# A fused attention and MLP kernel: the last 64 tokens of the first batch moved from the start into stage 2 of tile 0, and the first w_in transfer cut in halves

## The chip, the cores and the metric

The kernel runs on one core of one Trainium2 chip. The metric is the device time of one execution in microseconds (us). A ratio of a kernel is the mean time of its fast runs over the mean time of the fast runs of the kernel before in the same rounds on the same chip, so it is not quite the ratio of the medians that stand beside it; the brackets hold its 95% interval. The experiments ran on several chips, so I compare their ratios.

Engines: PE multiplies matrices (PEld is its weight load), DVE is VectorE, ACT is ScalarE, POOL is GpSimd, SP issues transfers. A transfer has *landed* when the last of its sixteen completions is recorded in the trace.

## The reference

```python
# q, k, v: (8 batches, 8 heads, 576 tokens, 64) f32; w_in: (512, 2048); w_out: (2048, 512)
scores = scale * np.matmul(q, k.transpose(0, 1, 3, 2))
mask = (rel >= 0) & (rel < 64)              # each token sees itself and the 63 before
...                                          # softmax
x = np.matmul(attn, v).transpose(0, 2, 1, 3).reshape(4608, 512)
h = x @ w_in
g = h * np.clip(h + 3.0, 0.0, 6.0) / 6.0
out = g @ w_out
```

The 4608 tokens are worked on in nine tiles of 512. Stage 1 of a tile is `x @ w_in` with the gate, stage 2 is the product with `w_out`. A batch has 576 tokens, 64 more than a tile: the last 64 tokens of batch 0 ("the rest") belong to tile 1.

## The kernel before

PE is given one fixed list of work, in which the attention of the next batch is laid between pieces of the two stages. Only the start and tiles 0 and 1 matter here.

```python
# loads of batch 0 by SP: q and k by pairs of heads, then the rest of q and k, then V
for h0 in range(0, H, 2):
    ...                                   # q, k of heads h0, h0 + 1, tokens 0:512
    if h0 == 2:                           # the rest: tokens 512:576 of all heads
        for i, src in enumerate((q, k)):
            nc.sync.dma_start(out=rst[i*SR:(i+1)*SR], in_=src[0, :, SM:S, :]...)
# POOL: casts to bf16, and w_in in four parts of 512 columns, which cast while they move
bt.cast_v_end(vst0, pcopy)
bt.cast_v(vst0, 0, 2, pcopy)
w_in = []
for i in range(4):
    w_in.append(load_w_in(512 * i, 512 * (i + 1), 0, NG))
    if i < 3:
        bt.cast_v(vst0, 2 * i + 2, 2 * i + 4, pcopy)
...
# w_out in four parts behind w_in; batch 1's V behind the third of them
for x in insv:
    after(x, w_out[2], "the weights go first")
...
# stage 2 of tile 0: m yields one piece (four matmuls 128x512) at a time
run(m, 2)
masked(bt, 3)
run(m, 2)
for g in range(NG):        # four pairs of heads of batch 1
    run(m, 1)
    N_(bt, g)              # value matmuls (PE), normalisation (DVE)
    run(m, 1)
    if g:
        X_(bt, g - 1)      # transposes (PE), copy into x (ACT)
run(m)
```

`SS(b, g)` in the list of pieces below stands for the scores of a pair of heads, with exponentials on ACT and the mask on DVE; the number in front is the piece of stage 2 after which it comes.

The softmax here doesn't subtract the row's maximum and nothing guards it: scores larger than these inputs give would overflow.

## Time and profile before

| | |
|---|---|
| time, median of 3 | 316.76 us (315.65 to 317.39) |
| span of the profiled execution | 312.9 us (its run took 314.71) |
| PE busy | 298.8 us, 96% |
| stage 1 of tile 0 starts, last w_out part landed | about 20.6 us, 46.68 us |
| stage 1 of tile 1 starts, stage 2 of tile 1 starts, stage 1 of tile 2 starts | 59.7, 74.3, 93.8 us |

The profile is read from the start: PE is full from 39 us on, so what counts is when its list of work gets to a place, and which transfer or copy it waits for there. The prediction shows the lines. The profiled execution was a quick one (314.71 us against a median of 316.76), so differences between traces come out about 1 us larger than those between medians.

### The profile page before, as it was taken

To read this page: it belongs to the slowest core of one execution; us is meant where nothing else is said; L and a number is where in the kernel's file an instruction comes from. 1 tells how busy PE (TensorE), PEld (TensorE's weight loads), DVE (VectorE), ACT (ScalarE), POOL (GpSimd) and SP (SyncE) were. 2 spreads that over 40 slices of the span, in tenths; PEclk is the share of its full clock that TensorE was granted. 3 is DMA by queue.
4 is the path that set the end of the run, shared out by engine and by line. 5 is a ranking of instruction groups with operands and counts; after the bars stand their busy time and mean duration, and the time that the engine had idled before them with its cause. 6 is when DMAs were issued, how large, how long until landed. Compare 5 with 4: busy or idle time off the path is not lost.

```text
span 312.9 us, 5589 instructions
## 1 busy us (share of the span) xinstructions
PE 298.8 (96%) x2126; PEld 149.0 (48%) x2162; DVE 174.5 (56%) x331; ACT 177.2 (57%) x264; POOL 86.1 (28%) x131
## 2 busy tenths in 40 slices
PE   7879799999999999999999999999999999999995
PEld 3444444544554455445544554455445544444442
DVE  4557753476646765477447853785377627306700
ACT  3648753378637854696158715881588157317611
POOL 5840805363036143306500750165000000000000
PEclk9999999999999999999999999999999999999998
DMA  8999999998899999999999999999900630010011
GB/s 212 241 180 250 250 203 196 205 185 245 187 195 212 272 214 205 229 228 216 195 248 202 207 199 239 212 198 186 242 4 2 128 93 0 34 69 34 0 69 67
DMA packets 151516, 52.80 MB, mean 169 GB/s; under 512 B 138945, under 2 KB 147137, under 8 KB 151489
## 3 DMA queue, kind: packets, MB, share of 16 engines
q1 hardware_dynamic: 146672, 46.94, 73.5%
q0 software_dynamic: 4544, 5.24, 9.2%
q8 instruction: 17, 0.28, 0.4%
q10 hardware_dynamic: 272, 0.26, 0.2%
q14 instruction: 11, 0.08, 0.1%
HBM read 36.70 MB, written 9.44 MB: 147 GB/s over the span
## 4 chain that ended last, share of the span: by engine, by line
PE 88%; ACT 3%; DMA 3%; SPq 2%; DVE 1%; issue 1%; POOL 1%
PE o L503 20%; PE acc L503 19%; PE hT L466 18%; PE st L466 8%; PE acc L466 6%; PE o L466 6%; PE st L347 4%; PE hT L377 2%; PE hT L382 2%; DMA qst<-in_q_dram 1%; PE hT L407 1%; DMA vst<-in_v_dram 1%; ACT pT L355 1%; DVE gT L474 1%; SPq L82 1%
## 5 line engine op out<-in xcount | busy, mean ns | idle before, releaser
L466 PEld LDWEIGHTS <-win 128*128 128x128 bf16 x576 | 55.4, 98 | 66.9 <-issue 1.0
L503 PEld LDWEIGHTS <-gT 128*128 128x128 bf16 x576 | 52.8, 98 | 57.6 <-issue 0.4
L503 PE MATMUL o<-wout,gT 128*128 128x512 bf16 x277 | 68.1, 379 | 0.8 <-issue 0.2
L503 PE MATMUL acc<-wout,gT 128*128 128x512 bf16 x275 | 66.1, 379 | 0.8 <-issue 0.2
L466 PE MATMUL hT<-xT,win 128*128 128x512 bf16 x267 | 64.9, 379 | 0.3
L355 ACT ACTIVATE pT<-st 128x768 bf16<-128x768 f32 x64 | 48.8, 810 | 15.1 <-PE st L347 15.0
L474 DVE SCALAR_TENSOR_TENSOR gT<-t,st 128x512 bf16<-128x512 bf16 (+1 forms) x26 | 19.7, 768 | 56.6 <-ACT t L473 56.5
L473 ACT ACTIVATE t<-hT,half 128x512 bf16<-128x512 f32 x68 | 46.1, 691 | 8.8 <-PE hT L466 8.6
L474 DVE SCALAR_TENSOR_TENSOR gT<-t,hT 128x512 bf16<-128x512 bf16 x68 | 46.0, 685 | 8.6 <-ACT t L473 8.4
L365 DVE TENSOR_TENSOR pT<-pT,mask 128x1536 bf16<-128x1536 bf16 x28 | 28.2, 1006 | 16.3 <-ACT pT L355 16.3
L252 POOL CAST qn<-qst 128x512 bf16<-128x512 f32 x24 | 15.7, 695 | 71.4 <-DMA qst<-in_q_dram 71.4
L509 ACT COPY osb<-acc 128x512 f32<-128x512 f32 x18 | 10.6, 587 | 39.2 <-PE acc L503 39.2
L509 ACT COPY osb<-o 128x512 f32<-128x512 f32 x18 | 10.6, 588 | 35.4 <-PE o L503 35.4
L466 PE MATMUL st<-xT,win 128*128 128x512 bf16 x116 | 27.9, 379 | 1.4 <-ACT xT L412 0.8
L397 DVE TENSOR_TENSOR opg<-hT,rec 128x320 bf16<-128x320 f32 x56 | 27.5, 492 | 1.9
L466 PE MATMUL acc<-xT,win 128*128 128x512 bf16 x91 | 23.6, 379 | 0.1
L466 PE MATMUL o<-xT,win 128*128 128x512 bf16 x90 | 23.5, 379 | 0.1
L473 ACT ACTIVATE t<-st,half 128x512 bf16<-128x512 f32 (+1 forms) x26 | 19.4, 752 | 6.0 <-PE st L466 5.9
L377 PEld LDWEIGHTS <-pT 128*128 128x128 bf16 x256 | 17.9, 97 | 9.6 <-issue 2.0
L394 DVE RECIPROCAL rec<-hT 128x5 f32<-128x5 f32 x56 | 10.6, 189 | 19.0 <-PE hT L386 18.8
L243 POOL CAST V<-vst 128x512 bf16<-128x512 f32 (+1 forms) x14 | 16.3, 1167 | 16.2 <-DMA vst<-in_v_dram 9.8
L347 PE MATMUL st<-QT,KT 64*128 64x192 bf16 (+2 forms) x320 | 17.9, 229 | 2.7 <-ACT KT L316 1.5
(76 smaller groups left out, 267.1 us busy)
## 6 DMA issues: line engine op xcount, KB each, us to landing
out_dram<-osb SPq DMA_DIRECT2D x32, 256.0 KB, 2.4
qst<-in_q_dram SPq DMA_DIRECT2D x28, 256.0 KB, 4.9
kst<-in_k_dram SPq DMA_DIRECT2D x27, 256.0 KB, 5.7
vst<-in_v_dram SPq DMA_DIRECT2D x24, 256.0 KB, 5.3
vst<-in_v_dram SPq DMA_DIRECT2D x24, 128.0 KB, 4.4
win<-in_moe_w_in_dram POOLq DMA_DIRECT2D x4, 512.0 KB, 7.8
wout<-in_moe_w_out_dram POOLq DMA_DIRECT2D x4, 512.0 KB, 8.5
qst<-in_q_dram SPq DMA_DIRECT2D x2, 512.0 KB, 5.3
```

What stands on the lines that cost most here:

```text
L243: copy(out=self.V[:, 0 : KB - 1, h0:h1, 0:D], in_=vst[:, 0 : KB - 1, h0:h1, :])
L252: pcopy(out=n[:, g, 0 : KB - 1, :, :].rearrange("p k h d -> p k (h d)"), in_=s[:, 0 : KB - 1, 2 * g : 2 * g + 2, :].rearrange("p k h d -> ...
L347: nc.tensor.matmul(st[:, h, o0 : o0 + n], lhsT=bt.KT[h * D : (h + 1) * D, g, k0 : k0 + P], rhs=bt.QT[h * D : (h + 1) * D, g, q0 : q0 + n], ...
L355: nc.scalar.activation(out=pT[:, :, 2 * u : 2 * u + 2, 0:QW], in_=st[:, :, 0:w].rearrange("p h (k w) -> p h k w", k=2), func=EXP, scale=scale,
L365: nc.vector.tensor_tensor(out=pT[:, :, :, 0:QW], in0=pT[:, :, :, 0:QW], in1=mask[:].rearrange("p (h k) w -> p h k w", h=2), op=MULT,)
L377: nc.tensor.matmul(ob, lhsT=pT[:, h, qb, 0:P], rhs=V[:, qb, 2 * g + h, :], start=True, stop=(qb == 0),)
L397: nc.vector.tensor_tensor(out=opgs[bt.b, g][:, :, h, :], in0=ov[:, :, 0:D], in1=rec[:].unsqueeze(2).to_broadcast([P, KB, D]), op=MULT,)
L466: nc.tensor.matmul(hT, lhsT=win16[:, g, fc * P : (fc + 1) * P], rhs=xT[:, g, t0 : t0 + TB], start=(g == 0), stop=(g == NG - 1),)
L473: nc.scalar.activation(out=t1[:], in_=hT, func=RELU, bias=half[:], scale=1.0 / 6.0)
L474: nc.vector.scalar_tensor_tensor(out=out, in0=t1[:], scalar=1.0, in1=hT, op0=MIN, op1=MULT,)
L503: nc.tensor.matmul(accs[ts], lhsT=gT[:, fc, ts * P : (ts + 1) * P], rhs=wout16[:, fc, :], start=(fc == 0), stop=(fc == NFC - 1),)
L509: nc.scalar.copy(out=osb[:], in_=accs[ts])
```

## The change

Its intent: stage 1 can start when the attention of batch 0 is done; without the last 64 tokens there are three loads, six casts and some matmuls fewer in front of it. The rest's attention is done later, in a place where PE works on stage 2 of tile 0. The first w_in part comes in two halves so that stage 1 can start with the first. The loads of batch 2 come later, so its scores do, too.

```diff
@@ loads of batch 0: the rest and the V tail leave the start @@
-            if h0 == 2:
-                for i, src in enumerate((q, k)):
-                    nc.sync.dma_start(out=rst[...], in_=src[0, :, SM:S, :]...)
+    def load_rest_of_first():        # issued in front of batch 1's V
+        for dst, p0, src in ((rst, 0, q), (rst, SR, k), (rvst, SR, v)): ...
@@ POOL at the start @@
-        if g == 1:
-            bt.cast_rest(st, pcopy)
-    bt.cast_v_end(vst0, pcopy)
     bt.cast_v(vst0, 0, 2, pcopy)
-    w_in = []
-    for i in range(4):
-        w_in.append(load_w_in(512 * i, 512 * (i + 1), 0, NG))
-        if i < 3:
-            bt.cast_v(vst0, 2 * i + 2, 2 * i + 4, pcopy)
+    bt.cast_v(vst0, 2, 4, pcopy)
+    w_in = [load_w_in(0, 512, 0, 2)]
+    bt.cast_v(vst0, 4, 6, pcopy)
+    w_in.append(load_w_in(0, 512, 2, NG))
+    bt.cast_v(vst0, 6, 8, pcopy)
+    w_in += [load_w_in(512 * i, 512 * (i + 1), 0, NG) for i in (1, 2, 3)]
@@ POOL in stage 2 of tile 0, in front of batch 1's V @@
+    bt0.cast_rest((None, None, rst0), pcopy)
+    pcopy(out=bt0.V[SR:P, KB - 1, :, 0:D], in_=rvst0[SR:P, :, :])
+    pcopy(out=bt0.V[0:SR, KB - 1, :, 0:D], in_=bt0.V[SR:P, KB - 2, :, 0:D])
     bt.cast_v_end(vst1, pcopy)
@@ PE in stage 2 of tile 0 @@
     masked(bt, 3)
-    run(m, 2)
+    later[0, "r"] = bt0.rest_t(...)      # 4 transposes
+    do(bt0, "r")
+    run(m, 1)
+    rest_s(bt0)                          # 8 score matmuls
     for g in range(NG): ...
+        if g == 0:
+            rest_n(bt0)                  # 8 value matmuls
+        if g == 1:
+            rest_x(bt0)                  # 4 transposes
@@ batch 2 in stage 2 of tile 1 @@
-                0: [f(SS, 0)], 1: [f(SS, 1)], 3: [f(N_, 0), f(SS, 2)], 5: [f(X_, 0)],
-                6: [f(N_, 1), f(SS, 3)], 8: [f(X_, 1)], 9: [f(N_, 2)], 11: [f(X_, 2)],
-                12: [f(N_, 3)], 14: [f(X_, 3)],
+                1: [f(SS, 0)], 2: [f(SS, 1)], 4: [f(N_, 0), f(SS, 2)], 6: [f(X_, 0), f(SS, 3)],
+                7: [f(N_, 1)], 9: [f(X_, 1)], 10: [f(N_, 2)], 12: [f(N_, 3), f(X_, 2, 0)], 14: [f(X_, 3, 1)],
... (removal of the rest from the matmuls of batch 0, other cuts)
```

## The prediction

> **What bounds the kernel now.** I read the page first, to see which engine fills the span.
>
> ```profile
> PE 298.8 (96%) x2126; PEld 149.0 (48%) x2162; DVE 174.5 (56%) x331; ACT 177.2 (57%) x264; POOL 86.1 (28%) x131
> PE   7879799999999999999999999999999999999995
> ```
>
> TensorE (PE) is busy 96% of the span. Its only slices (7.8 us each) under 9 tenths are four of the first five and the last. So from about 39 us on the end can move only if PE's whole stream starts earlier or loses gaps; time is to be had at the start. There I read the chain of waits in order of time.
>
> ```profile
> 3.72 0.04 issue
> 3.76 4.53 DMA qst<-in_q_dram
> ...
> 11.88 3.75 DMA vst<-in_v_dram
> 15.63 0.70 POOL win L222
> ...
> 18.19 0.63 POOL V L243
> ...
> 18.86 0.22 PE o L377 x2
> ...
> 19.97 0.65 ACT xT L412
> 20.62 0.16 issue
> 20.78 1.67 PE st L466 x7
> ```
>
> Up to 20.8 us the end is set by loads of q, then of v, then by GpSimd (POOL), which casts V and issues the w_in loads in turn. L466 is the first matmul of stage 1 of tile 0; from there the chain is PE. The list of waits adds what the chain hides: the weight load of that matmul waited for w_in itself. The chain shows seven matmuls there where the program has eight, so one record is missing, and I take 20.55, where the timeline has the weight load, as the start.
>
> ```profile
> PEld L466 <- DMA win<-in_moe_w_in_dram: 0.8, 1, 0.8
> ```
>
> Then I asked whether the DMA engines have room, by stretches of the start.
>
> ```profile
> 2.00:45.00 43.00, 37.08 (x331) 19.52 (x333) 26.58 (x64) 26.53 (x40) 20.43 (x32) 1.00 1.15 234
> ```
>
> The last two numbers are the DMA share and GB/s. A share of 1.15 over 43 us means that they never rest before 45 us. So everything up to the last w_out load is one queue of bytes, and I checked how closely PE follows it. The last w_out is issued at 37.88, and the view of that tile gives:
>
> ```profile
> DMA to landing us min/median/max: 7.0/8.5/8.8
> ```
>
> With the largest it lands at 46.7. PE begins the part that reads it (u=3 of the first block) at 46.76 in the timeline. The third part has landed by 44.02, when SP issues batch 1's V, which waits for it; PE uses it at 44.48. PE is at the heels of the weights.
>
> **What the Trainium skill says.** "DMA: Bandwidth & Descriptors", Specifications: transfers under 512 B fall short of line rate. The trace agrees: between 8 and 9 us, with 1 KB runs of q and k, 351 GB/s; between 12 and 13 us, with 256 B runs of v, 219. The last 64 tokens are loaded in 256 B runs, so each of their three loads (131 KB) costs about 0.6 us of the DMA engines. Same page, "Issuing engines are not separate DMA queues": all queues run on the same 16 engines. So a load that moves is not saved; it delays what it is put in front of. "Runtime: NRT & Kernel Launch", Instruction fetch mechanics: instructions arrive in 16 KiB blocks of 256. The page agrees (instruction queue: 17 packets, 0.28 MB). PE's third fetch here is at 46.8 us, and SP's issue of a V load at 46.98 then took 1.74 us instead of 0.51; a fetch can hit the new loads. "TensorE: Matmul & The Clock Gate", part 2: only weight loads are pulled ahead, matmuls stay in order. The trace shows the same, so a rest matmul that waits holds everything behind it.
>
> **The change part by part.**
> (1) Loads. Out of the start go two rst loads and the V tail: 3 x 131 KB / 219 GB/s = 1.8 us of DMA time, and 0.73 + 0.62 + 0.61 us of SP's issue. The third q pair, issued at 3.76, goes out at 2.32; V follows it. V should land 1.8 us earlier.
> (2) POOL. The casts of rn (0.62) and V's end (0.61) and the four half-tile casts (0.29 each) leave: 2.4 us. The last V cast, 18.19 before, falls to about 15.5 (V data 1.8 earlier, one 0.3 tail less per round, and each w_in issue of 0.75 still between casts).
> (3) PE, VectorE and ScalarE of the start: per head pair one score pair, two of 16 value matmuls and one of 5 transposes fewer, and normalisation over 256 columns instead of 320 (0.49 to about 0.4). None was the last wait; four rounds of about 1.2 us from the first V cast put PE at the door of stage 1 at about 17.4.
> (4) w_in in halves. Before, the first part was issued at 13.72 and landed in 6.8 us. V's data end near 13.5-14 now; half a moves half the bytes, about 1.3 us less, so it lands near 17.5 and half b near 19.2, in time for the (2,) group. Stage 1 starts about 2.9 us earlier. But parts 1, 2, 3 are now all issued after the last V cast, and behind them the stream is earlier only by about 1.25 us: 1.8 us of bytes less what the later issues and the slow start of the software queue lose.
> (5) What becomes of the 2.9. Batch 1's first heads (cast waiting for w_in part 2, then k at 32.4), then w_out 0 to 3, all ride on the stream, so PE catches up with it: w_out 1 would be needed at 41.55 - 2.4 = 39.2 and lands near 40.2. By the last w_out, where there was no slack (46.7 against 46.76), PE's gain is the stream's: X = 1.25 us, between 0.8 and 1.8.
> (6) The rest in stage 2 of tile 0. PE work: 4 transposes 0.3, 8 scores 0.27, 8 value matmuls 0.27, 4 transposes 0.15, together 0.9 to 1.0 us, inserted where PE is the path (the same work removed at the start was not). Waits: the casts of rst0 end about 4.9 us after w_out 2 (two loads at 3.5 and 4.1 us, cast 0.62), PE wants them at 4.55: 0.35 lost, against 0.25 before at the same spot for the o bank. Batch 1's V comes three loads (1.8 us) later while PE reaches N(0) with two pieces done instead of three: 0.2 to 1.2 us lost. To the good: one piece of stage 2 is left for the last head pair, which closes the 0.39 us wait on the xT copy at 58.76 and some of the other 0.8 us of stalls there. Net: about +0.5 us (-0.1 to +1.3).
> (7) Batch 2's loads are behind the three new ones: 1.8 - 1.25 = about 0.6 us later than before. K's transpose of pair 0 landed at 74.8 and PE wanted it at 75.28. One piece (0.86 us) later it is wanted as late as it comes; no stall over 0.3. The last transposed outputs taking the score banks are neutral.
> After that PE's stream is the same.
> Sum: -1.25 + 0.5 = -0.75, so 316.76 - 0.75 = 316.0.
>
> **The rivals.**
> - *The whole start is kept* (2 to 3 us faster, near 314). For it: stage 1 does start that much earlier. Against: the DMA share of 1.15 to 45 us, and w_out landing 0.1 us before use.
> - *The rest's loads take the gain back or more* (317 to 318). For it: V of batch 1 was cast from 49.92 (waiting 1.72 us for its data) for a use at 51.33, so little slack absorbs 1.8 us of loads; a fetch may add 1.2 to 2 us to one load. Against: PE has its own work between, and N(1) to N(3) come later than their casts.
> - *POOL starves the DMA queues*: with V's last pair hit by a fetch, parts 1 to 3 of w_in are issued a microsecond later and a gap opens; X falls to 0.8 or less and PE waits in stage 1 at its fifth block. Time about 316.5.
>
> **Range and chances.** X's spread of 0.5 and the insertion's 0.6 make about 0.8; the three runs before spread 315.65 to 317.39, which adds 0.6 to a median. An 80% range of 1.3 to 1.4 either side: 314.6 to 317.3. Two per cent is 6.3 us, which nothing here reaches: faster 0.01, within 2% 0.98, slower 0.01.
>
> **What would show it.** Right: L466's first matmul at about 17.6 instead of 20.6; a new PE wait for w_in part 1 or w_out 0/1 in stage 1 or at the start of stage 2; the last w_out landing near 45.4 instead of 46.7; the rn0 cast within half a microsecond of PE's wish; stage 1 of tile 1 starting at about 59.0 instead of 59.7; from there the same stream. Wrong: w_out landing 2 us or more earlier (then the first rival), a PE wait over 1.5 us for V or rn0 in stage 2 (the second), a DMA share under 1 between 14 and 20 us (the third), or a stall at batch 2's scores over 0.5 us.

## The result and the profile after

The kernel after takes 319.99 us in the median (319.07 to 320.56, 4 runs) against 316.72 us (315.65 to 317.39, 4 runs): ratio 1.0104 [1.0063, 1.0144]. It is about 3.3 us slower, outside the predicted range of 314.6 to 317.3 us. Executions over 1.5% slower than the fastest of the same kernel are left out of the means. The profiled execution has a span of 317.2 us (run 319.07).

The top of the page hardly shows it:

```profile
PE 301.3 (95%) x2125; PEld 148.7 (47%) x2162; DVE 176.4 (56%) x336; ACT 178.2 (56%) x266; POOL 87.5 (28%) x129
PE   7879699999989999999999999999999999999995
PEclk9999989999999999999999999999999999999999
```

PE is busy 2.5 us longer, though it has no more work. The last row is its granted clock, and the 8 in the sixth slice means that the clock was reduced for a part of it; before, only the last slice had an 8. I come back to this.

The chain of waits up to the start of stage 1 of tile 1, in order of time (start, duration, what):

```profile
15.76 9.59 DMA win<-in_moe_w_in_dram
...
27.15 6.69 DMA rst<-in_k_dram
...
35.24 9.55 DMA wout<-in_moe_w_out_dram
...
46.14 3.45 DMA rvst<-in_v_dram
...
49.70 0.62 POOL V L727
50.37 1.12 POOL V L728
...
51.66 0.62 POOL V L252
52.34 0.62 POOL V L247
53.04 0.35 POOL V L249
53.44 0.19 PE hT L394
```

Before, no transfer and no POOL operation stood in this chain from 20.8 us on; it was PE with some steps of ACT and DVE, and came to the first value matmuls of batch 1 so:

```profile
48.74 2.75 PE o L503 x12
51.49 0.06 PE hT L377 x2
```

Now it runs through w_in, batch 1's own loads and w_out until 44.8 us, then through the load of the rest's V (rvst) and five operations of POOL, of which the first two (L727, L728) are the rest's, to a value matmul of batch 1 at 53.44. The last transfer named (rvst) and the first two casts are work that the change put there.

Next, where the stream of weights lost its time. Busy time by microsecond (the last three numbers of a line are granted clock, DMA share and GB/s), after and then before:

```profile
14.00:15.00 1.00, 0.98 (x22) 0.68 (x22) 0.43 (x3) 1.00 (x2) 1.00 (x2) 1.00 0.79 109
15.00:16.00 1.00, 0.54 (x13) 0.45 (x14) 0.93 (x5) 0.60 (x2) 1.00 (x3) 1.00 1.01 132
16.00:17.00 1.00, 0.81 (x18) 0.55 (x15) 0.96 (x4) 0.52 (x1) 1.00 (x2) 1.00 0.90 97
17.00:18.00 1.00, 0.87 (x13) 0.69 (x15) 0.93 (x4) 0.39 (x2) 0.26 (x1) 1.00 1.08 119
18.00:19.00 1.00, 1.00 (x6) 0.45 (x5) 0.96 (x5) 0.26 (x1) 0.00 (x0) 1.00 0.67 80
20.00:21.00 1.00, 0.75 (x4) 0.40 (x5) 0.00 (x0) 0.27 (x1) 0.00 (x0) 1.00 1.25 209
```

```profile
16.00:17.00 1.00, 0.44 (x11) 0.36 (x8) 0.93 (x4) 0.94 (x2) 0.84 (x2) 1.00 0.98 140
17.00:18.00 1.00, 0.84 (x20) 0.76 (x20) 0.53 (x3) 0.11 (x1) 0.94 (x3) 1.00 1.15 189
18.00:19.00 1.00, 0.36 (x10) 0.28 (x7) 0.96 (x3) 0.64 (x1) 0.89 (x3) 1.00 1.15 170
```

After the change, from 14 to 19 us, only w_in is moving, and it moves at 80 to 132 GB/s where the same queue does some 205 from 20 us on. (These are bytes as written, in bf16.) Before, where its first packets come at 15.3 us, the queue starts slowly too (140), but is at 170 to 189 two microseconds later; after, it takes five. PE then waits for w_in in stage 1, in the list of waits up to 40 us (total us, times, longest):

```profile
PEld L524 <- DMA win<-in_moe_w_in_dram: 2.0, 2, 1.2
...
PE hT L524 <- DMA win<-in_moe_w_in_dram: 0.7, 1, 0.7
```

These two rows overlap in part, since PE and its weight load wait together. The view of the w_out tile after ends with the line that answers to the one in the prediction:

```profile
DMA to landing us min/median/max: 7.7/8.8/9.8
```

The transfers' times in us:

| | before | after | after minus before |
|---|---|---|---|
| stage 1 of tile 0 starts | 20.6 | 17.75 | -2.8 |
| first w_in part landed | 20.50 | 17.47 and 20.20 (halves) | -0.3 |
| w_in parts 2, 3, 4 landed | 23.01, 25.61, 28.15 | 22.79, 25.35, 27.89 | -0.2, -0.3, -0.3 |
| last w_out part landed | 46.68 | 47.40 | +0.7 |
| stage 1 of tile 1 starts | 59.7 | 62.7 | +3.0 |
| stage 2 of tile 1 starts | 74.3 | 77.6 | +3.3 |
| stage 1 of tile 2 starts | 93.8 | 98.0 | +4.2 |
| end | 312.9 | 317.2 | +4.3 |

So stage 1 of tile 0 starts as early as predicted, and by the last w_out part all is lost. Another 2.3 us go between that and stage 1 of tile 1, and 1.0 in stage 2 of tile 1. (One matmul record of eight is missing at the start of stage 1 of tile 1 before, so it began some 0.2 us earlier than 59.7; what seems lost in the stage itself is that.) From 98 us on the two traces run side by side.

The POOL timeline of stage 2 of tile 0, before and after (start, duration, line, operation, out and in, what it waited for):

```profile
49.92 0.62 POOL L243 CAST V<-vst 128x512 bf16<-128x512 f32 x1 [1.72 <-DMA vst<-in_v_dram]
```

```profile
48.93 0.61 POOL L293 CAST rn<-rst 128x512 bf16<-128x512 f32 x1 [8.77 <-DMA rst<-in_k_dram]
49.70 0.62 POOL L727 CAST V<-rvst 64x512 bf16<-64x512 f32 x1 [0.16 <-DMA rvst<-in_v_dram]
50.37 1.24 POOL L728 COPY V<-V 64x512 bf16<-64x512 bf16 x1
51.66 0.61 POOL L252 CAST V<-vst 64x512 bf16<-64x512 f32 x1
52.34 0.62 POOL L247 CAST V<-vst 128x512 bf16<-128x512 f32 x1
```

Before, POOL waited for the data; batch 1's first V cast began at 49.92. After, the data of that pair has landed at 51.42, but POOL has not got through the rest's three operations and the end of V; the cast begins at 52.34.

Stage 2 of tile 1, after: the timelines of DVE and of PE.

```profile
88.69 0.96 DVE L371 TENSOR_TENSOR pT<-pT,mask 128x1536 bf16<-128x1536 bf16 x1 [1.86 <-ACT pT L361]
89.57 0.19 DVE L402 RECIPROCAL rec<-hT 128x5 f32<-128x5 f32 x1
...
90.42 0.49 DVE L405 TENSOR_TENSOR opg<-hT,rec 128x320 bf16<-128x320 f32 x1
```

```profile
90.97 0.45 PE L416 MATMUL hT<-ident,opg 128*128 128x128 bf16 x5 [1.00 <-DVE opg L405]
```

DVE masks the fourth pair's scores, for which it waited for ACT's exponentials until 88.69, and only then normalises the second pair, whose value matmuls PE had finished before. PE's transposes wait 1.00 us. In the order of before the fourth scores stood behind those value matmuls; there is no such wait in that trace.

From these views I had three theories: (A) the halves slow the queue; (B) the insertion costs 2 to 2.5 us, mostly through POOL and the loads in front of batch 1's V; (C) the place of the fourth scores costs 1 us. The rivals were that POOL's issues are late, that one copy of 1.24 us is the cost, and, from the clock row, that a slow PE clock is.

### The profile page after: what moved, and what is told of

It is laid out like the page before. It is cut to its first block, busy times and chain, and to the rows that moved or that the text cites.

```text
span 317.2 us, 5591 instructions
## 1 busy us (share of the span) xinstructions
PE 301.3 (95%) x2125; PEld 148.7 (47%) x2162; DVE 176.4 (56%) x336; ACT 178.2 (56%) x266; POOL 87.5 (28%) x129
## 4 chain that ended last, share of the span: by engine, by line
PE 78%; DMA 12%; POOL 2%; ACT 2%; SPq 2%; DVE 2%; issue 2%; POOLq 0%
PE acc L561 18%; PE o L561 17%; PE hT L524 17%; PE acc L524 6%; PE o L524 6%; PE st L524 5%; PE st L353 3%; DMA win<-in_moe_w_in_dram 3%; DMA wout<-in_moe_w_out_dram 3%; DMA rst<-in_k_dram 2%; PE hT L383 2%; PE hT L388 1%; DMA qst<-in_q_dram 1%; DMA rvst<-in_v_dram 1%; PE hT L416 1%
## 5 line engine op out<-in xcount | busy, mean ns | idle before, releaser
L561 PE MATMUL o<-wout,gT 128*128 128x512 bf16 x276 | 68.8, 382 | 1.0 <-issue 0.5
L371 DVE TENSOR_TENSOR pT<-pT,mask 128x1536 bf16<-128x1536 bf16 x28 | 29.1, 1040 | 17.9 <-ACT pT L361 17.8
L531 ACT ACTIVATE t<-st,half 128x512 bf16<-128x512 f32 (+1 forms) x26 | 19.4, 752 | 7.1 <-PE st L524 7.1
L383 PEld LDWEIGHTS <-pT 128*128 128x128 bf16 x256 | 17.6, 97 | 8.7 <-issue 0.9
L247 POOL CAST V<-vst 128x512 bf16<-128x512 f32 (+1 forms) x14 | 16.4, 1168 | 15.7 <-DMA vst<-in_v_dram 12.8
L257 POOL CAST kn<-kst 128x512 bf16<-128x512 f32 x24 | 14.9, 658 | 19.1 <-DMA kst<-in_k_dram 19.1
L353 PE MATMUL st<-QT,KT 64*128 64x192 bf16 (+2 forms) x312 | 17.6, 230 | 1.9 <-ACT KT L321 1.5
```

The costliest lines, as they stand in the source:

```text
L247: copy(out=self.V[:, 0 : KB - 1, h0:h1, 0:D], in_=vst[:, 0 : KB - 1, h0:h1, :])
L257: pcopy(out=n[:, g, 0 : KB - 1, :, :].rearrange("p k h d -> p k (h d)"), in_=s[:, 0 : KB - 1, 2 * g : 2 * g + 2, :].rearrange("p k h d -> ...
L353: nc.tensor.matmul(st[:, h, o0 : o0 + n], lhsT=bt.KT[h * D : (h + 1) * D, g, k0 : k0 + P], rhs=bt.QT[h * D : (h + 1) * D, g, q0 : q0 + n], ...
L371: nc.vector.tensor_tensor(out=pT[:, :, :, 0:QW], in0=pT[:, :, :, 0:QW], in1=mask[:].rearrange("p (h k) w -> p h k w", h=2), op=MULT,)
L383: nc.tensor.matmul(ob, lhsT=pT[:, h, qb, 0:P], rhs=V[:, qb, 2 * g + h, :], start=True, stop=(qb == 0),)
L531: nc.scalar.activation(out=t1[:], in_=hT, func=RELU, bias=half[:], scale=1.0 / 6.0)
```

## The experiments

All gave correct results. Each edit is shown against the kernel that is named. Several expectations missed the time: whole gained more and halves_only cost more than forecast, and no gain came that could be told from noise in after_warm, after_ss3, rest_v_late, rest_v_warm and rest_v_warm_ss3.

| kernel | median us (runs) | before | ratio |
|---|---|---|---|
| whole | 317.1 (6) | 316.43 | 1.0024 [1.0009, 1.0039] |
| old_scores | 318.24 (6) | 316.43 | 1.0071 [1.0052, 1.0091] |
| copy_early | 318.65 (6) | 316.43 | 1.0094 [1.0065, 1.0124] |
| halves_only | 319.51 (5) | 316.43 | 1.0113 [1.0094, 1.0132] |
| whole_old | 316.48 (6) | 316.61 | 0.9997 [0.9958, 1.0037] |
| after_warm | 320.05 (6) | 316.61 | 1.0113 [1.0067, 1.0158] |
| late_half | 318.94 (6) | 316.61 | 1.0065 [1.0023, 1.0107] |
| rest_v_late | 317.12 (6) | 316.61 | 1.0016 [0.9971, 1.0061] |
| rest_v_warm | 316.77 (6) | 316.33 | 1.0016 [0.9976, 1.0056] |
| before_warm | 316.47 (6) | 316.33 | 1.0002 [0.9961, 1.0042] |
| halves_in_a_row | 319.28 (6) | 316.33 | 1.0098 [1.0048, 1.0149] |
| halves_by_columns | 319.21 (6) | 316.33 | 1.0081 [1.0042, 1.0121] |
| first_in_quarters | 319.63 (4) | 316.44 | 1.0107 [1.0084, 1.0130] |
| second_in_halves | 318.97 (4) | 316.44 | 1.0093 [1.0061, 1.0125] |
| halves_then_two | 319.97 (4) | 316.44 | 1.0120 [1.0092, 1.0147] |
| rest_v_warm_ss3 | 316.52 (22) | 316.44 | 1.0010 [0.9990, 1.0030] |
| scores_only | 317.33 (22) | 316.41 | 1.0031 [1.0013, 1.0048] |
| after_ss3 | 319.26 (6) | 316.41 | 1.0095 [1.0066, 1.0124] |

### The halves of the first w_in part

**whole** (against after) and **halves_only** (against before):

```diff
# whole                                          # halves_only: the change's POOL order
-    w_in = [load_w_in(0, 512, 0, 2)]
+    w_in = [load_w_in(0, 512, 0, NG)]
     bt.cast_v(vst0, 4, 6, pcopy)
-    w_in.append(load_w_in(0, 512, 2, NG))
```

(halves_only is before with the seven lines of the change from `cast_v(vst0, 2, 4)` to `w_in +=`, and nothing else. These lines also move the issues behind the casts of V.)

> The changed kernel with the first w_in part whole again, issued where half a was (after the second V cast). Theory A (the two halves are what makes the software queue crawl between 14 and 19 us, at some 110 GB/s where it later moves 205): the DMA share from 14 to 19 us is above 1.1, w_in part 2 lands near 24 instead of 25.35 us, stage 1 has no wait for w_in over 0.3 us after its start, the start of stage 1 is at 18.5 to 19.5 instead of 17.7; the time falls by 0.5 to 1.3 us against the changed kernel, to about 319. Theory B (the crawl is from the three w_in issues in a row, or from the cold queue): the share stays under 1.1 for 4 us or more, part 2 lands at 25 or later, and the time is that of the changed kernel, 320, within 0.5.

> The kernel before with only the w_in part of the change: first part in two halves, issued after the second and third V cast, parts 1 to 3 after the fourth. Theory A (halves make the software queue crawl): DMA share under 1.1 for 4 us after the first w_in packets, w_in part 2 lands later than 25.6 us, by 0.5 to 1.5 us, PE waits for w_in in stage 1, time 317.0 to 318.2. Theory B (halves are harmless): part 2 lands at 25.6 within 0.4, time 316.3 to 317.0.

The windows of whole:

```profile
14.00:15.00 1.00, 1.00 (x23) 0.75 (x22) 0.43 (x3) 1.00 (x2) 0.95 (x2) 1.00 0.62 71
15.00:16.00 1.00, 0.53 (x11) 0.38 (x11) 0.96 (x4) 0.68 (x2) 1.00 (x2) 1.00 1.24 208
18.00:19.00 1.00, 1.00 (x6) 0.49 (x5) 0.96 (x5) 0.33 (x1) 0.00 (x0) 1.00 1.24 207
```

The queue is at full rate from 15 us on, with the same casts on POOL around the issues. The whole first part landed at 17.73, hardly later than the first half in after; stage 1 started at 17.77, PE's weight load waited 0.2 us for w_in in all, and the last w_out landed at 45.10, 1.6 us earlier than before. This is the best of the traces with a whole first part: in five others of the kernels below the part landed at 18.1 to 19.1 us and PE's weight load waited up to 1.3 us for w_in, so a little was there for the halves to win. Theory A is shown, and larger than I had put down. Between whole and after lie 0.8 of a per cent, 2.5 us, with intervals that do not meet; old_scores and whole_old below, which also differ in nothing but the halves, lie 0.74 of a per cent apart, 2.3 us. The traces agree: the last w_out landed at 47.1 to 48.6 us in all nine kernels with the change's start and a split first part, and at 45.1 to 46.3 in whole, whole_old, rest_v_late and rest_v_warm (47.5 in rest_v_warm_ss3, where one completion of the first part came late).

halves_only (1.0113) cannot show the halves alone. In its trace POOL waited 1.25 us for V in front of the second half, issued at 18.18 us, and the second, third and fourth parts were issued at 19.88 to 21.4 us; before, these issues began at 15.57, 17.40 and 19.11. So its loss holds the later issues too.

Why the halves are slow was tried in six kernels. **late_half** puts the *last* w_in part of whole in halves; **halves_in_a_row** issues the two halves of after together, in front of the cast that stood between; **halves_by_columns** cuts them as 256 columns of all rows; **first_in_quarters** makes four transfers of it; **second_in_halves** has the first part whole and the second in halves; **halves_then_two** has four transfers in all.

```diff
# late_half (against whole)
-    w_in += [load_w_in(512 * i, 512 * (i + 1), 0, NG) for i in (1, 2, 3)]
+    w_in += [load_w_in(512 * i, 512 * (i + 1), 0, NG) for i in (1, 2)]
+    w_in += [load_w_in(1536, 2048, 0, 2), load_w_in(1536, 2048, 2, NG)]
# halves_in_a_row (against after)
     w_in = [load_w_in(0, 512, 0, 2)]
-    bt.cast_v(vst0, 4, 6, pcopy)
     w_in.append(load_w_in(0, 512, 2, NG))
+    bt.cast_v(vst0, 4, 6, pcopy)
# halves_by_columns (against after)
-load_w_in(0, 512, 0, 2)   load_w_in(0, 512, 2, NG)
+load_w_in(0, 256, 0, NG)  load_w_in(256, 512, 0, NG)
# first_in_quarters (against after): at each place of a half two of
+load_w_in(0, 512, g, g + 1)
# second_in_halves (against whole)
+    w_in += [load_w_in(512, 1024, 0, 2), load_w_in(512, 1024, 2, NG), ...]   # then parts 3, 4;
+        after(x, w_in[3], ...)                        # batch 1's loads behind part 3, as in whole
# halves_then_two (against after)
+    w_in += [load_w_in(512, 1536, 0, NG), load_w_in(1536, 2048, 0, NG)]
```

> The kernel whole with the fourth w_in part, the last one issued, in two halves in place of the first. Theory shape: a transfer of half the rows is slow by itself; then the fourth part lands a us or more later than 25.41 us, the DMA engines move less than 200 GB/s while it runs, and the time is 318 us or more. Rival, start: halves are slow only while the queue is empty and the casts of V go on between the issues; then both halves have landed by about 25.4 us at 205 GB/s and the time is that of whole, 317.1 us within 0.4.

> The kernel after with both halves of the first w_in part issued in a row, at the place of the first. Theory: the halves are slow because the queue runs empty and starts again between two issues with a cast of V between them; then both have landed by 18.2 us, the rate between 15 and 19 us is over 180 GB/s, and the time falls to that of whole, about 317.3 us. Rival: a transfer of half the rows is slow by itself, at the start more than late in the queue (late_half: 0.7 us in 3.3); then the second half lands at 19.5 us or later at some 100 to 130 GB/s and the time stays at 319 us or more.

> The kernel after with the two halves of the first w_in part cut by columns (all four row groups, 256 columns each) in place of by rows, issued at the same two places. It moves the same bytes in as many packets as a whole part's count, each of half the size. If it is the number of transfers and the place of their issues that slows the queue, they crawl as in after (the second half landing at 20 us or later). If it is that a transfer has too few rows, it runs near 200 GB/s and the second half lands by 18.5 us. Pieces of half the size may take longer by themselves, which the records of the packets would show.

> The kernel after with the first w_in part in four transfers of a quarter each, two where each half was issued. If at the start a transfer takes a fixed time of some 2.7 us whatever it holds, the four land at about 17, 20, 22.5 and 25 us, and the time grows by some 5 us, to about 325. If it is a low rate while the first part runs (105 to 130 KB per us), the last quarter lands at about 20.2 us as the second half did, and the time stays near 320 us. In between: each further boundary costs about 1 us, 22 us and 322 us.

> The kernel whole with the second w_in part in halves in place of the first, issued in a row where the second was. If only the head of an empty queue is slow, the second half lands about 2.7 us after the first part, near 20.5 us, and the rate stays near 205 KB per us: 317.1 us within 0.5. If halves are slow at any place of the start, it lands at 22.5 us or later and the time is about 319 us. late_half has shown 0.7 us for a pair at the end of the queue.

> The kernel after with the first part in halves and the second and third parts in one transfer, so four transfers in all, as in before and whole. If five transfers in the queue are what slows it, the halves land at about 16.5 and 18 us and the time falls towards 317.3 us. If it is the halves themselves, the second lands at about 20 us as in after and the time stays at 319 to 320 us.

| kernel | landings of the pieces of the part, us | from the landing (or start) in front |
|---|---|---|
| after | 17.47, 20.20 | second half 2.73 after the first |
| halves_in_a_row | 17.07, 19.82 | 2.75 |
| halves_by_columns | 16.20, 19.31 | 3.11 |
| halves_then_two | 16.84, 19.79 | 2.95 |
| first_in_quarters | 15.99, 17.54, 18.19, 19.66 | 3.67 for the last three quarters |
| second_in_halves | 21.50, 22.77 | 4.44 for the whole part, from the first part's 18.33 |
| late_half | 26.14, 27.43 | 3.25 for the whole part, from 24.18 |
| whole, its second part | 20.27 | 2.54 for the whole part |

What follows: it is not the cast between the issues (in a row: the same), not the cut (columns: the same), not a fixed time for each transfer (four quarters end when two halves do), and not the number of five transfers (four: the same). It is not only the head of an empty queue, since the second part in halves lost 1.1 to 1.9 us (4.44 against 2.54 in whole, up to 3.3 in other kernels) and the last lost 0.7. A first part of a megabyte that is split costs 2 to 3 us at the start of this queue, whatever the split. (These are landings of one execution each. Among the kernels with after's own w_in lines, the second half came 2.3 to 2.9 us after the first, so differences of 0.5 us between the rows of the first part mean nothing.) What the engines do in that time stays open; I could not tell it from the packet records, in which single packets last up to 1.2 us instead of 0.1 at 16 to 18 us.

### The order of batch 2's pieces

**old_scores** is after with before's order; **scores_only** is before with the change's order; **after_ss3** moves only the fourth scores:

```diff
# after_ss3 (against after)
-   6: [f(X_, 0), f(SS, 3)], 7: [f(N_, 1)], ...
+   6: [f(X_, 0)], 7: [f(N_, 1), f(SS, 3)], ...
```

> The changed kernel with the order of batch 2's pieces in stage 2 of tile 1 as before (scores at pieces 0, 1, 3, 6; no score banks for transposed outputs). Theory A (the new order puts the mask of head pair 3 in front of the normalisation of pair 1 in VectorE's queue, and X(1) two pieces later waits 1.0 us for it): no PE gap over 0.5 us before a transpose in stage 2 of tile 1; if K's transposes come in time the time falls by 1.0 us to about 319.0. Rival (the batch's transposes really come as late as the change assumes): PE waits at the first scores for the DMA transpose, 0.8 us or more, and the time is 319.5 to 320.5.

> The kernel before with nothing but the change's order of batch 2's pieces (and the last two transposed outputs in the score banks). Theory: the mask of the fourth pair goes on VectorE in front of the second pair's normalisation and PE waits 1.0 us for it in stage 2 of tile 1, whatever the start does; then from the start of stage 2 of tile 1 to that of stage 1 of tile 2 it takes 20.4 us in place of 19.5 and the time is 317.3 us, 0.7 to 1.2 us over before. Rival, as in the prediction: neutral, within 0.3 us of before.

> The kernel after with the fourth scores of batch 2 behind the second pair's value matmuls, all else of the change's order kept. Theory: the wait of 1.0 us is gone as in old_scores, that stretch takes 19.5 to 19.7 us, and the time is 0.8 to 1.2 us under after, about 319 us. Rival: it is the transposed outputs in the score banks or the later first scores that cost; then the stretch stays at 20.4 us.

| | ratio | stage 2 of tile 1 to stage 1 of tile 2 |
|---|---|---|
| before | | 19.4 us |
| after | 1.0104 | 20.4 us |
| old_scores | 1.0071 | 19.7 us |
| scores_only | 1.0031 [1.0013, 1.0048] | 20.4 us |
| after_ss3 | 1.0095 | 19.4 us |

In scores_only, where nothing else is changed, the list of waits of that stretch has the wait at its top:

```profile
PE hT L407 <- DVE opg L397: 0.8, 1, 0.8
```

Theory C is shown: the order costs about 1 us by itself, and the place of the fourth scores is the cause, since the stretch is back at 19.4 us when they alone are moved. All eleven traces with the change's order have 20.4 us there. The time of after_ss3 is not told apart from that of after (its profiled execution also had the last w_out 1.0 us later, at 48.44), so the proof is in the stretch and not in the ratio.

The old order is not free either, which the trace of before alone does not show: in before_warm and halves_only, with before's order, the same stretch took 20.4 and 20.5 us, because PE waited 0.9 and 1.0 us for the transposed K of batch 2. The later first scores of the change avoid this wait; only its fourth scores stand wrong.

### The insertion

**whole_old** is whole with before's order of batch 2, so that only the shorter start and the insertion are left. **copy_early** is after with the copy of L728 done when POOL idles. **rest_v_late** is whole_old with the rest's V behind the first V loads and casts of batch 1, the copy early, the rest's last two steps one pair later, and one transposed output in a score bank.

```diff
# rest_v_late (against whole_old), POOL and PE; the load of rvst moves behind four V loads likewise
+    pcopy(out=bt0.V[0:SR, KB - 1, :, 0:D], in_=bt0.V[SR:P, KB - 2, :, 0:D])   # behind the last w_out issue
     bt0.cast_rest((None, None, rst0), pcopy)
-    pcopy(out=bt0.V[SR:P, KB - 1, :, 0:D], in_=rvst0[SR:P, :, :])
-    pcopy(out=bt0.V[0:SR, KB - 1, :, 0:D], in_=bt0.V[SR:P, KB - 2, :, 0:D])
     bt.cast_v_end(vst1, pcopy)
     for g in range(NG):
         bt.cast_v(vst1, 2 * g, 2 * g + 2, pcopy)
+        if g == 1:
+            pcopy(out=bt0.V[SR:P, KB - 1, :, 0:D], in_=rvst0[SR:P, :, :])
...
-            X_(bt, g - 1)
-        if g == 0:
+            X_(bt, g - 1, 1 if g == 3 else None)
+        if g == 1:
             rest_n(bt0)
-        if g == 1:
+        if g == 2:
             rest_x(bt0)
```

> The changed kernel with GpSimd's copy of 64 rows of V inside SBUF (1.24 us, between the cast of rvst and the casts of batch 1's V) moved up to right after the last w_out issue, where GpSimd idles. Theory A (GpSimd's row of casts is what N(0) of batch 1 waits for): its first V cast ends 1.0 to 1.2 us earlier, the PE wait before N(0) shrinks from about 0.7 to under 0.2, stage 1 of tile 1 starts about 0.7 us earlier, time 319.3. Rival (the loads of batch 1's V are the bound): the wait moves to the V loads, the gain is under 0.3 us.

> The kernel after with the first w_in part whole and batch 2's pieces in the order of before, so that of the change only the start without the last 64 tokens and their insertion in stage 2 of tile 0 are left. If the costs found so far add up (halves 2.9 us, order of the scores 1.0 to 1.7 us), it takes 317.1 - 1.0 to 1.7 = 315.4 to 316.1 us, the wait of 1.0 us in stage 2 of tile 1 is gone, and what is left against the kernel before is the insertion, which then has eaten the whole gain of the start. Rival: the order of the scores only costs where the stream is late already; then it stays at 317.1.

> whole_old with the load and the cast of the last 64 tokens' V put behind the first two pairs of batch 1's V, the copy of V rows done early while GpSimd idles, the value matmuls and transposes of the rest one head pair later, and the transposed outputs of the third pair put in a score bank. Theory: the insertion costs what it does because GpSimd's three casts and the three loads stand in front of batch 1's V and because two banks are short at the end; then PE's first value matmul of batch 1 comes at 49.3 to 49.9 us in place of 50.8, the wait of 0.6 us before the third pair's transposes is gone, and the time is 1.2 to 1.8 us under whole_old, 314 to 315 us, below the kernel before. Rival: the 1.0 us of PE work and the slow clock before stage 2 are what costs; then it is within 0.5 us of whole_old.

The copy alone changed little (1.0094 against after's 1.0104, with the intervals over each other): inconclusive, and at most a part. whole_old is level with before, so the insertion eats all that the start wins.

Its size is best read as the time from the landing of the last w_out part to stage 1 of tile 1. PE does not always use that part at once, so the third column says how long after the landing it did; the fourth counts from the first value matmul of batch 1.

| kernels | last w_out landed to stage 1 of tile 1 | landed to first use | first value matmul to stage 1 |
|---|---|---|---|
| without the insertion: before, before_warm, halves_only, scores_only | 13.0, 13.1, 12.8, 12.7 us | 0.1, 0.4, 0.1, 0.0 | 8.4, 8.2, 8.2, 8.4 |
| with it: after, whole, whole_old, old_scores, halves_in_a_row, halves_then_two | 15.3, 15.3, 15.7, 15.3, 15.3, 15.3 us | 1.1, 0.5, 1.3, 1.0, 1.1, 1.3 | 9.7 in all |
| rest_v_late | 15.1 us | 2.1 | 8.8 |
| rest_v_warm | 13.3 us | 0.2 | 8.8 |
| rest_v_warm_ss3 | 15.0 us | 1.8 | 8.8 |

So the insertion costs some 2.5 us (2.2 to 2.6 in most pairs of these traces), the same in kernels that come to it at 45.1 and at 48.6 us. Of this, 1.3 to 1.6 us come after the first value matmul of batch 1 (before and scores_only lack one matmul record there, so their 8.4 is 0.2 too long). In whole, whose trace waits most clearly there, 0.9 us are PE waiting for batch 1's V, 0.6 the last transposes waiting until DVE has normalised a head of the fourth pair and so freed a bank (their own data had been ready for 1.9 us), and about 1 us the inserted work. This split is one trace's: in after and whole_old PE waited only 0.2 us for V, and came later to w_out instead.

In rest_v_late both waits are gone from the list of waits, and the last column falls to 8.8 us, so the new places work. Still the first column says 15.1 us, because PE came to the last w_out part 2.1 us after it had landed. The windows of the time ahead of that, and of rest_v_warm below, for the same eight us:

```profile
36.00:44.00 8.00, 6.67 (x30) 2.70 (x31) 1.56 (x2) 3.40 (x6) 2.43 (x3) 0.57 1.22 203
```

```profile
36.00:44.00 8.00, 7.21 (x58) 3.79 (x61) 2.70 (x4) 4.47 (x8) 2.34 (x3) 1.00 1.18 197
```

The seventh quantity is the granted clock: 0.57 on the mean with 30 matmuls done, against 1.00 with 58.

### The clock of PE

In after the clock drops to 0.50 from 39.0 us, behind three microseconds in which PE was busy 0.81 (36 to 37), 0.10 and 0.56 us:

```profile
37.00:38.00 1.00, 0.10 (x4) 0.11 (x4) 0.00 (x0) 1.00 (x3) 0.04 (x1) 1.00 1.24 207
...
39.00:40.00 1.00, 0.47 (x5) 0.47 (x6) 1.00 (x2) 0.26 (x1) 1.00 (x2) 0.50 1.25 209
```

**after_warm**, **before_warm** and **rest_v_warm** put spare matmuls in two waits ahead of stage 2 of tile 0, in after, before and rest_v_late:

```diff
     do(bt, "s", 0, 0)
+    spare(ps_st.tile([P, 2, 512], F32, name="st1")[:, 0, :], 4)   # four matmuls 128x512, result unused
     S_(bt, 0, 1)
...
+        if g == 1:
+            spare(ps_o.tile([P, 512], F32, name="o")[:], 4)
         if g + 1 < NG:
             T_(bt, g + 1)
```

> The kernel after with two times four matmuls of 128x512 that compute nothing needed, put in front of two waits of PE before stage 2 of tile 0 (one of 1.0 us for the copy of K, one of 0.97 us for the cast of k). In the trace of after PE is busy 0.10, 0.56 and 0.47 us of the three us from 37 on, and then the granted clock is 0.50 for about 3.3 us; a mean clock of 0.995 goes with runs of 319.1 and 319.4 us, 0.989 with 320.6 us. Theory: the idle stretch halves the clock and this costs 1 to 2 us; with the spare matmuls the clock stays at 1.00 in most runs and the time falls to 318 to 319 us. Rival: in that stretch PE would wait for w_out anyway, and the clock costs nothing; then 319.5 us or more, or above 320 if the spare matmuls are in the way.

> Control: the kernel before with the same spare matmuls at the same two places. Its executions have a mean clock of 1.00 or 0.995 at times that hardly differ, so the spare matmuls should gain at most 0.3 us: 316.4 us within 0.5. If it is a us or more faster, what rest_v_warm gains is owed to the spare matmuls and not to the change.

> rest_v_late with the two times four spare matmuls of after_warm. In rest_v_late PE waits nowhere over 0.3 us from 39.0 us to the start of stage 1 of tile 1 at 61.4, 22.3 us, but the granted clock is 0.50 for about 6.7 us of it, and eleven matmuls of 128x512 come at steps of 0.43 us in place of 0.22. Theory: where PE is the path, as here, the halved clock costs all it takes away, 2 us; with the clock at 1.00 the stretch is 20 to 20.5 us and the time 315 to 316 us, below the kernel before by up to 1 us. Rival: PE then waits for w_out, whose last part landed at 46.3 us, and for the casts of V, as after_warm did; then within 0.5 us of rest_v_late, about 317 us.

In after_warm the clock was at 0.999 or more in five of six runs, and the time did not fall (1.0113). The trace shows where it went: PE then used the last w_out part 0.05 us after its landing and not 1.07, but waited 1.1 us for the cast of the rest's q and k, and its first value matmul, which needs V, came no earlier (8.3 us after the third w_out part, 8.2 in after). So in after the slow clock is largely beside the path, and my theory for after found no support; the interval, 1.4 us either way, does not exclude a small part. In rest_v_late, where those waits are gone, PE is the path, and there the clock counts: with the spare matmuls PE came to the last w_out part 0.2 us after its landing in place of 2.1, and the stretch fell from 15.1 to 13.3 us. From the start of stage 2 of tile 0 to stage 1 of tile 1 it took 22.8 us in rest_v_late and 20.9 in rest_v_warm, and 20.5 in rest_v_warm_ss3 below, which has the spare matmuls too but started stage 1 late. These are three traces, one of each. before_warm (1.0002 [0.9961, 1.0042]) shows no gain from the spare matmuls by themselves.

And yet rest_v_warm is no faster than rest_v_late against before (1.0016 both). It reached stage 2 of tile 1 at 73.6 us, 0.7 earlier than before, and waited there:

```profile
PE st L355 <- DMA KT<-kn: 1.8, 1, 1.8
```

That is the transposed K of batch 2, whose loads did not come earlier. **rest_v_warm_ss3** has the change's order of batch 2 (first scores one piece later) with the fourth scores behind the second value matmuls.

> rest_v_warm with the change's order of batch 2's pieces, but the scores of the fourth pair behind the value matmuls of the second pair in place of in front of them. In rest_v_warm PE reaches stage 2 of tile 1 at 73.6 us and then waits 1.8 us for the transposed K of batch 2, because it is earlier than before while the loads are not. Theory: the first two scores one piece (0.86 us) later take about 0.9 us off this wait, and with the fourth scores behind, the wait of 1.0 us for the normalised outputs of the second pair, which the change's order had, does not come; then 315.3 to 316.2 us, at or a little below the kernel before. Rival: the piece that is put in front only moves the wait elsewhere; then 316.8 us as rest_v_warm.

That wait is gone from its trace, and the stretch takes 19.4 us. Its time is 1.0010 [0.9990, 1.0030], with 22 runs from 314.99 to 319.57 us: level with before. Its profiled execution shows one thing that can spread the runs: of the sixteen completions of the first, whole w_in part fifteen came from 17.77 to 18.22 us and the last at 20.66 (in whole all came from 17.28 to 17.73), and stage 1 started at 21.1 us. In that execution one late completion took away the start's whole gain. No kernel that I ran beats the kernel before.

## Why the prediction was wrong

The prediction was 316.0 us, and 319.99 came. It summed -1.25 (the stream), +0.5 (the insertion) and nothing for the order.

**Parts (1) to (3), right in what they lead to.** Stage 1 of tile 0 starts at 17.75 us (17.6 expected), though the last V cast came at 14.45 us and not at 15.5. That the weights bound what can be kept was right, too: with whole parts, in whole, whole_old, rest_v_late and rest_v_warm, the last w_out landed 0.4 to 1.6 us earlier than before, around the 1.25 of the prediction.

**Part (4), wrong; this is the largest term.** The step that failed is "half b near 19.2, in time" and "behind them the stream is earlier only by about 1.25 us". I priced a half by its bytes: half the bytes, so 1.3 us less. Measured, the second half landed at 20.20, 2.7 us after the first, and the last w_out landed 0.7 us *later* than before: 2.0 us off the sum; whole against after puts the cost of the halves at 2.5 us. A reading went wrong ahead of it: "they never rest before 45 us" was taken from a mean share of 1.15 over 43 us, while the trace of before has shares of 0.99 and 0.98, and 88 and 140 GB/s, between 15 and 17 us, where w_in starts. The Trainium skill had a warning that I did not use: "DMA: Bandwidth & Descriptors", Bandwidth, gives as a rule to batch transfers to at least 1 MiB for 75% of peak. A whole part reads 512 x 512 x 4 B, 1.05 MB, a half 0.52 MB. The traces agree in direction for the start (80 to 132 GB/s against 205) but not as a law of size: late in the queue a pair of halves lost 0.7 us only, and quarters lost no more than halves.

**Part (5), right in that the stream sets it, wrong in its number**, which it took from part (4): X was not +1.25 but -0.7. And PE was not at the heels of the last w_out part any more: it used it 1.1 us after the landing (0.1 before), which is counted in part (6) here.

**Part (6), wrong in size.** "Net: about +0.5 us (-0.1 to +1.3)" was some +2.5 (2.3 in after), much the same in six kernels. PE's 1 us of work was right. The waits were under-priced: I took 0.2 to 1.2 for V and counted the freed piece of stage 2 as a gain that closes the stalls at the last pair. In whole V cost 0.9 us (in after 0.2, where PE came later), and the last transposes wait 0.6 us for a bank instead of being relieved: the freed piece was used up ahead of the last value matmuls, so nothing stood behind them. I had also counted loads, and not that POOL has three more operations in a row in front of V.

**Part (7), wrong.** I looked at when the transposed K lands and found no stall; in after there was none. The stall came from the other end: "later" also put the fourth scores in front of the second value matmuls, and on DVE a mask that waits for ACT then stands in front of a normalisation that PE waits for. It is about 1 us, shown alone in scores_only. The score banks for the last outputs, which I had called neutral, are in after_ss3 with a stretch of 19.4 us, so that part holds.

Together: 2.0 (stream) + 1.8 to 2.1 (insertion) + 1.0 (order) = 4.8 to 5.1 us, which turn -0.75 into about +4.0 to +4.4; the two traces differ by 4.3 us, the medians by 3.3.

**The rivals.** The third named the right sign, a DMA share under 1 between 14 and 20 us (0.67 to 1.08 was measured until 19 us, 1.21 after that), with the wrong cause: POOL issued all five transfers by 17.3 us, with no wait for V's data in between. The second, that the rest's loads take the gain back, is what is left once the halves are undone: whole_old is level with before. The range was too narrow because it had only the spread of the terms that I had thought of.

## What to carry to other kernels

Before you cut a transfer in two so that work can start on the first half, ask what the second half does to everything behind it; here the first half had landed (17.47 us) just as PE came to it (17.52), and the stream behind paid 2 to 3 us. When a piece of work is moved, walk the queue of *each* engine in its new place: of the two costs, the insertion and the order, only about 1 us was the moved matmuls themselves; the rest came with POOL's casts, DVE's mask, a bank that was not free and the loads in front of V, in the order in which they now stood. And a gain at the start is kept only as far as every later arrival is earlier too: here w_out, batch 1's V and batch 2's K each took their share back in turn.

## What the Trainium skill lacked or had wrong

- "DMA: Bandwidth & Descriptors" has a rule on the size of a transfer, but nothing on pieces in a queue that starts: one part of 1.05 MB in two or four pieces ran at 57 to 150 GB/s (as written) for some 5 us and had landed at 19.2 to 20.2 us in nine kernels, where it landed at 17.7 to 19.1 us in one piece in six (20.7 in a seventh, with one late completion); the same pair late in the queue lost only 0.7 us. Cut, spacing of the issues and number of pieces made little difference.
- The same page calls two of the sixteen engines usually slower, but has no figure for the lag of single engines: the sixteen completions of the first w_in part, whole, lay within 0.45 us in one execution; in another fifteen did and the last came 2.4 us behind them, and the parts behind it had their last completion 1.4 us late, too.
- "TensorE: Matmul & The Clock Gate", Part 1, ties the halved clock to an idle window of about 3.4 us. Here PE was not idle that long: it was busy for 1.47 of the three us ahead of the drop in after (0.81, 0.10, 0.56), and the clock was at 0.50 for 3.4 us, in rest_v_late for 6.8. The kernel before with 1.84 of three us (0.93, 0.64, 0.27) kept 1.00. The page's "A second HAM failure mode" has short idle times doing the same, but what share of work is enough is not said. In the traces PE was busy for 23 to 58% of the 3.4 us ahead of each of the fourteen drops up to 48 us, while six other such stretches with 53 to 59% kept 1.00 (the record changes only at steps of 3.41 us, and the stretches are counted in these steps). That a halved clock costs next to nothing where PE waits for data anyway (after_warm 1.0113, after 1.0104) is not said there either.
- No page has the case of the order on VectorE, where a mask that waits for ScalarE holds up a normalisation behind it; it cost 0.8 to 1.0 us of PE's time.
